# Reordering the start of a fused attention and FFN kernel: first loads, score tiles, one eviction and the weight slices

## The chip, the cores and the metric

The kernel runs on one core of a Trainium2 chip. The core has TensorE (PE in the profile; PEld is its weight load), VectorE (DVE), ScalarE (ACT), GpSimd (POOL) and SyncE (SP). Work between them is ordered by semaphores; each engine runs its own list in order. DMAs are issued by SP, ACT and POOL and are moved by 16 DMA engines. The metric is the device time of one execution in microseconds, median over runs. All times below are microseconds unless said otherwise; positions are counted from the start of the profiled span.

## The reference

The inputs are q, k, v of shape (8 batches, 12 heads, 448 positions, 64) and three weights. Attention uses a sigmoid in place of a softmax, and its output feeds a gated FFN:

```python
scores = (1 / sqrt(64)) * (q @ k.T) - log(448)
attn   = sigmoid(scores)
x      = (attn @ v) laid out as (8 * 448 tokens, 12 * 64 = 768)
g      = x @ w_gate                       # 768 -> 1536
out    = (g * sigmoid(g)) * (x @ w_val) @ w_out   # 1536 -> 768
```

The output is (3584, 768) in float32.

## The kernel before

**Groups and tiles.** The work of attention is cut into 24 groups n: batch n // 3, and four heads each. For one group the kernel loads q, k and v, casts q and k to bf16 (`cast`, L204; for the parts of group 0 `cast_part`, L174), transposes them in seven pieces of 128 columns on PE against an identity (`trans_part`, L223) and copies them from PSUM to SBUF (the tiles `T` and `Tk`, L229). Later groups are transposed by DMA instead. The keys of a group form seven chunks c. For each tile (n, c), `qk_tile` (L254) makes the scores of 64 keys by 448 queries for four heads, four matmul instructions on 64x64 weights, and `sig_tile` (L273) runs one sigmoid over 128 x 896 of them on ACT into `pt_a`. `chunk(n, c)` is both. When all seven tiles of a group exist, `pv(n)` multiplies them with V (L289, 28 matmuls) into one PSUM slot and evicts the slot to the FFN's input `xT`: bank 0 by one copy on DVE (L304), bank 1 by two copies that swap partition halves (L312).

**PSUM.** All of PSUM is a ring of four slots of two banks (`ring`, taken by `Banked`). A slot goes to the next user in the order in which the program asks, unless `at` names one; the new user's matmuls wait until the last reader of the former user is done. So a score tile has to wait for the sigmoid of the tile four uses earlier, and whoever follows a `pv` in a slot has to wait for its evictions.

**FFN.** `ffn1_mm` (L324) multiplies weights with `xT`, gate into bank 0, value into bank 1; each output column block f takes six products for each of the two. The weights come in four column slices, `wg` and `wv` 0 to 3, each for three blocks f. At the end of the ramp three blocks are begun early (`early[0]` to `early[2]`) with the four of six `xT` tiles that the first two groups give; the other two come from `pv(2)`. After that a planner's list alternates FFN1 blocks, attention visits of the next groups and, later, the third matmul. The list is the same before and after.

**The ramp's order.** Everything up to the early FFN1 blocks is written out by hand at the end of the function, one call after another, and each engine's list follows it. The four part loads of group 0 come first (`load_part`; q in pieces 0 to 3 and 4 to 6, k in pieces 0 to 1 and 2 to 6), then the loads of groups 1 to 3 on SP. Eight matmuls on a zero tile keep PE busy meanwhile (L814). Then the casts and transposes of group 0, chunks (0,0) and (0,1), the transposes of the second part of k, and so on; `trans_pe(n)` transposes a whole group and copies it on DVE.

**POOL's queue.** POOL issues the DMAs that change the type (V, the weight slices) and some loads of q and k (`load(n, which, G)`), and casts q and k of group 4 on (`casts`). It does this in program order, so a cast that waits for its load holds up the DMAs written behind it. `plan` lists such calls for later visits; the entry (3, 2) is carried out after tile (3, 2).

The ramp's slots come out as follows. Slots 0 and 1 hold the transposes of group 0; then tiles (0,0) to (0,5) take 2, 3, 0, 1, 2, 3; group 1's transposes 0; (0,6) 1; (1,0) 2; (1,1) 3; (1,2) 0; `pv(0)` 1; (1,3) 2; (1,4) 3; group 2's transposes 0; (1,5) 1; (1,6) 2; (2,0) 3; (2,1) 0; `pv(1)` 1; (2,2) 2; group 3's transposes 3; (2,3) 0; then (2,4) 2, `early[0]` 1, (2,5) 0, `early[1]` 3, (2,6) 2, `pv(2)` 0, `early[2]` 2.

Of the kernel before, what the change touches and what calls it, by code (L numbers as in the profile page):

```python
# [20 lines left out]
def kernel(  # L21
# [10 lines left out]
    nc = tc.nc  # L32
# [5 lines left out]
    C = S // D  # L38
# [35 lines left out]
    ring_at = [0]  # L74
# [42 lines left out]
    def apart(second, *firsts):  # L117

        for first in firsts:
            keys[0] += 1  # L120
            tc.add_to_no_dep_group(f"half{keys[0]}", first.ins)
            tc.declare_no_dep(second.ins, group=f"half{keys[0]}", reason="another bank or other partitions")
# [8 lines left out]
    def w_load(kind, i):  # L131
        cs = slice(i * FW * 128, (i + 1) * FW * 128)
        if kind == "o":
            rows = moe_w_out[i // 2 * 2 * FW * 128:(i // 2 + 1) * 2 * FW * 128, :]
            nc.gpsimd.dma_start(out=wo16[i], in_=rows.rearrange("(f h p) n -> h p f n", h=2, p=128)[i % 2])
        else:
            w, dst = (moe_w_gate, wg16[i]) if kind == "g" else (moe_w_val, wv16[i])
            nc.gpsimd.dma_start(out=dst, in_=w[:, cs].rearrange("(j p) n -> p j n", p=128))
# [23 lines left out]
    def load_part(n, which, eng, lo, hi):  # L162

        st = osp.tile([128, DM], FP32, tag="osb", name=f"st{which}_{n}_{lo}")[:, :2 * (hi - lo) * D]
        st = st.rearrange("p (h x) -> p h x", h=2)
        eng.dma_start(out=st, in_=src_of(n, which)[:, :, lo * D:hi * D])  # L166
        qkv_st[(n, which, lo)] = st
# [21 lines left out]
    def load_v(n):  # L189
        t = v16p.tile([128, 2, S], FP16, tag="v16", name=f"v16_{n}")  # L190
        if flip(n):
            b, j = divmod(n, NJ)
            src = v[b, 4 * j:4 * j + 4].rearrange("h (p c) d -> p h (c d)", c=C)
            for w, heads in enumerate((slice(0, 4, 3), slice(1, 3))):
                nc.gpsimd.dma_start(out=t[w * 64:(w + 1) * 64], in_=src[:, heads])
        else:
            nc.gpsimd.dma_start(out=t, in_=src_of(n, 2))
        v16[n] = t

    def cast(n, which, eng):  # L200
        st = qkv_st.pop((n, which))
        t = c16.tile([128, C, 2, D], BF16, tag="c16", name=f"c16_{which}_{n}")
        q16[(n, which, 0)] = t
        eng.tensor_copy(  # L204
            out=t.rearrange("p c h d -> p h c d"), in_=st.rearrange("p h (c d) -> p h c d", c=C)
        )
# [10 lines left out]
    def trans_part(D2, bank, n, which, lo, hi, eng, d):  # L217

        t = q16.pop((n, which, lo))
        ps = D2.t.bitcast(BF16).rearrange("p w (c i) -> p w c i", c=8)  # L220
        for c in range(hi - lo):
            D2.write(
                nc.tensor.transpose(out=ps[:, bank, c, :], in_=t[:, c].rearrange("p h d -> p (h d)"), identity=idn),  # L223
                bank,
            )

        def copy():
            f = eng.copy if eng is nc.scalar else eng.tensor_copy
            D2.read(f(out=d, in_=ps[:, bank, :hi - lo, :]), bank)  # L229
            for c in range(lo, hi):  # L230
                qT[(n, which, c)] = d[:, c - lo]

        return copy

    def trans_pe(n):
        D2 = Banked()
        ds = [qkT.tile([128, C, 128], BF16, tag=f"T{w}", name=f"T{w}_{n}") for w in range(2)]
        for f in [trans_part(D2, w, n, w, 0, C, nc.vector, ds[w]) for w in range(2)]:
            f()
        qT[(n, 0)] = ds[0]  # L240
# [5 lines left out]
    def qk_tile(n, c, at=None):  # L246
        sd = Banked(at=at)
        sc = sd.t
        qt, kt = qT[(n, 0)], qT[(n, 1, c)]
        for w in range(2):  # L250
            for h2 in range(2):
                r = slice(h2 * 64, h2 * 64 + 64)
                g = (w ^ (h2 and flip(n))) * 64
                nc.tensor.matmul(  # L254
                    out=sc[g:g + 64, h2, :S],
                    lhsT=kt[r, w * 64:(w + 1) * 64],
                    rhs=qt[r, :, w * 64:(w + 1) * 64],
                    start=True,
                    stop=True,
                )  # L260
        return sd

    def sig_tile(n, c, sd, split=False):
        sc = sd.t
        pt = pt_a[:, pt_at[0] % 10]
        pt_at[0] += 1
        if split:
            for h2 in range(2):
                sd.read(
                    nc.scalar.activation(out=pt[:, h2, :], in_=sc[:, h2, :S], func=SIGM, bias=sbias, scale=qkscale), h2  # L270
                )
        else:
            nc.scalar.activation(out=pt, in_=sc[:, :, :S], func=SIGM, bias=sbias, scale=qkscale)  # L273
        pts[(n, c)] = pt

    def pv(n, how=0, at=None):

        b, j = divmod(n, NJ)
        P = Banked(at=at).t
        vt = v16.pop(n)  # L280
        for c in range(C):
            pt = pts.pop((n, c))
            for h2 in range(2):
                for w in range(2):
                    r, g = w * 64, (w ^ h2) * 64
                    if flip(n):
                        r, g = g, r
                    r = slice(r, r + 64)
                    nc.tensor.matmul(  # L289
                        out=P[g:g + 64, h2, :S],  # L290
                        lhsT=vt[r, h2, c * D:(c + 1) * D],
                        rhs=pt[r, h2, :],
                        start=(c == 0),
                        stop=(c == C - 1),
                    )

        def x_tile(h2):
            if n >= NQ - NJ:
                at = 4 * W2 + (2 * j + h2) * S
                return half_of(stg_a)[:, at:at + S]  # L300
            return xtp.tile([128, S], FP16, tag="xT", name=f"xT_{b}_{2 * j + h2}")

        xs = [x_tile(h2) for h2 in range(2)]
        first = nc.vector.tensor_copy(out=xs[0], in_=P[:, 0, :S])  # L304
        pairs = [(xs[1], P[:, 1, :S])] if flip(n) else [
            (xs[1][w * 64:(w + 1) * 64, :], P[(1 - w) * 64:(2 - w) * 64, 1, :S]) for w in range(2)
        ]
        for o, i in pairs:
            if how == 2:
                apart(nc.scalar.copy(out=o, in_=i), first)  # L310
            else:
                nc.vector.tensor_copy(out=o, in_=i)  # L312
        for h2 in range(2):
            xT[(b, 2 * j + h2)] = xs[h2]

# [3 lines left out]
    def ffn1_mm(D, b, f, prs, banks=(0, 1)):  # L319
        cs = slice((f % FW) * 128, (f % FW) * 128 + 128)  # L320
        for i in banks:
            for pr in prs:
                D.write(
                    nc.tensor.matmul(  # L324
                        out=D.t[:, i, :S], lhsT=(wg16, wv16)[i][f // FW][:, pr, cs], rhs=xT[(b, pr)],
                        start=(pr == 0), stop=(pr == NP - 1),
                    ),
                    i,
                )
# [447 lines left out]
    for grp in visits:  # L777
        n, c = grp[0]
# [3 lines left out]
        else:  # L782
            at = n + (0.5 if c else 0.0)
# [19 lines left out]


    QS, KS = 4, 2
    load_part(0, 1, nc.scalar, 0, KS)
    load_part(0, 0, nc.sync, 0, QS)
    load_part(0, 0, nc.sync, QS, C)
    load_part(0, 1, nc.sync, KS, C)
    for n, which in ((1, 0), (1, 1), (2, 0), (2, 1), (3, 0), (3, 1)):  # L810
        load(n, which)
# [1 line left out]
    for i in range(8):  # L813
# [4 lines left out]
    dk = [qkT.tile([128, n, 128], BF16, tag=f"Tk{n}", bufs=1, name=f"Tk{n}") for n in (KS, C - KS)]  # L818
    dq = qkT.tile([128, C, 128], BF16, tag="T0", name="T0_0")
    Dk, Dq = Banked(), Banked()  # L820
    trans_part(Dk, 0, 0, 1, 0, KS, nc.scalar, dk[0])()
    copies = [
        trans_part(Dq, 0, 0, 0, 0, QS, V, dq[:, :QS]),
        trans_part(Dq, 1, 0, 0, QS, C, V, dq[:, QS:]),
    ]
    for f in copies:
        f()
# [39 lines left out]
    def chunk(n, c, at=None):  # L867
        sig_tile(n, c, qk_tile(n, c, at))
# [12 lines left out]
    w_load("v", 1)  # L881
    load(4, 0, G)
    load(4, 1, G)
    load_v(3)
    for c in range(2, 6):
        chunk(0, c)
    trans_pe(1)
# [2 lines left out]
    chunk(0, 6)  # L890
    for c in range(3):
        chunk(1, c)
    pv(0)
    chunk(1, 3)
    chunk(1, 4)
    trans_pe(2)
    cast(3, 0, V)
    cast(3, 1, V)
    load(5, 0, G)
    load(5, 1, G)  # L900
    load_v(4)
    w_load("g", 2)
    chunk(1, 5)
    chunk(1, 6)
    chunk(2, 0)
    chunk(2, 1)
# [1 line left out]
    chunk(2, 2)  # L908
    trans_pe(3)
    casts(4)  # L910
    w_load("v", 2)
    load_v(5)
    w_load("g", 3)
    w_load("v", 3)
    chunk(2, 3)
# [1 line left out]
    k0 = ring_at[0] % 4  # L917
# [4 lines left out]
    ffn1_mm(early[0], 0, 0, range(3), (0,))  # L922
    chunk(2, 5, at=(k0 + 3) % 4)
    ffn1_mm(early[0], 0, 0, (3,), (0,))
    ffn1_mm(early[0], 0, 0, four, (1,))
    chunk(2, 6, at=(k0 + 1) % 4)
    ffn1_mm(early[1], 0, 1, four, (0,))
    pv(2, how=2, at=(k0 + 3) % 4)
    ffn1_mm(early[1], 0, 1, four, (1,))
# [2 lines left out]
    for f, Df in enumerate(early):  # L932
# [5 lines left out]

    post = []
    plan = {  # L940
        (3, 2): ((casts, 5), (post.append, 4)),
        (3, 4): ((post.append, 5),),
        (4, 0): ((fetch, 6),),
        (4, 4): ((ready, 6), (load_qk, 7), (load_qk, 8)),
# [102 lines left out]
```

## Time and profile before

| | us |
|---|---|
| median of 4 runs | 399.98 (399.53 to 400.93) |
| the profiled execution's own time | 400.42 |
| its span (first to last instruction) | 398.5 |
| PE busy in the span | 388.4 (97%) |
| DVE busy | 251.5 (63%) |
| ACT busy | 237.3 (60%) |
| POOL busy | 124.0 (31%) |
| first FFN1 product | 22.15 |
| granted TensorE clock, mean of the span | 0.995 |

The profile is of one execution. A line of the chain gives the start, the length and what it is; a line of a timeline gives start, length, engine, line of the program, operation, output<-input, and in brackets the idle time before it with what ended it. A line of busy time by stretch gives the stretch and its length, the busy time and (x) instruction count of PE, PEld, DVE, ACT and POOL, then the granted clock, the share of the DMA engines' time and GB/s. Matmuls are pipelined and their ends are modelled, so a busy PE is not PE at its peak.

### The profile page before, as it was taken

The page shows a single profiled execution, that of the slowest core. Times are in us where ns is not written, and L with a number is a line of the kernel's source. Part 1 is how long each engine was busy: PE and PEld are TensorE (multiplying, and loading weights), DVE is VectorE, ACT ScalarE, POOL GpSimd, SP SyncE. Part 2 cuts the span into 40 slices and gives each one's busy share as a digit, 9 for nine tenths or more (in the row PEclk, how much of TensorE's full clock was granted, in tenths as well). Part 3 has the DMA queues.
Part 4 walks back from the last instruction along what each step waited for, and adds up shares of the span by engine and source line. Part 5 has one row for each costly group of instructions (what it writes and reads, how often), then busy time and mean ns, then how long its engine had stood idle before and what let it go on. Part 6 is the DMA issues. An engine that isn't in the chain of part 4 may idle for free.

```text
span 398.5 us, 8117 instructions
## 1 busy us (share of the span) xinstructions
PE 388.4 (97%) x3110; PEld 202.7 (51%) x3110; DVE 251.5 (63%) x504; ACT 237.3 (60%) x385; POOL 124.0 (31%) x204
## 2 busy tenths in 40 slices
PE   6899999999999999999999999999999999999995
PEld 2545445444555444444455555455556655555663
DVE  2737646688643454466675554799986558787553
ACT  4966795746466797779772557966653065656000
POOL 3639042421311353333337538600007400000900
PEclk9899999999999999999999999999999999999999
DMA  8999989997599777798778699000000520000055
GB/s 262 253 245 257 244 174 227 185 180 116 137 286 232 172 164 163 163 187 163 165 162 200 102 195 243 17 2 1 1 2 0 160 79 2 2 2 0 2 171 146
DMA packets 65590, 54.39 MB, mean 137 GB/s; under 512 B 36048, under 2 KB 61744, under 8 KB 65552
## 3 DMA queue, kind: packets, MB, share of 16 engines
q1 hardware_dynamic: 49264, 37.04, 38.1%
q0 software_dynamic: 15376, 15.34, 24.5%
q10 hardware_dynamic: 912, 1.51, 1.2%
q8 instruction: 24, 0.39, 0.4%
q14 instruction: 14, 0.11, 0.1%
HBM read 47.19 MB, written 11.01 MB: 146 GB/s over the span
## 4 chain that ended last, share of the span: by engine, by line
PE 93%; DMA 3%; DVE 2%; issue 0%; SPq 0%; ACT 0%; DVEq 0%
PE ps_D L324 31%; PE ps_D L633 23%; PE ps_D L460 22%; PE ps_D L254 9%; PE ps_D L289 8%; DMA out_dram<-osb 2%; DMA st<-in_k_dram 1%; PE ps_D L223 1%; DVE xT L312 0%; DVE T L229 0%; DVE xT L304 0%; DVE osb L646 0%; SPq L166 0%; DVE stg_a L646 0%; ACT pt_a L270 0%
## 5 line engine op out<-in xcount | busy, mean ns | idle before, releaser
L273 ACT ACTIVATE pt_a<-ps_D 128x896 f16<-128x896 f32 x148 | 127.2, 921 | 42.4 <-PE ps_D L254 40.8
L324 PE MATMUL ps_D<-xT,wg 128*128 128x448 f16 x312 | 69.0, 353 | 0.2
L324 PE MATMUL ps_D<-xT,wv 128*128 128x448 f16 x312 | 68.5, 352 | 0.0
L349 DVE TENSOR_TENSOR t<-ps_D,s 128x448 f16<-128x448 f32 x52 | 32.4, 624 | 54.4 <-ACT s L347 53.6
L470 ACT ACTIVATE snap<-ps_D 128x448 f32<-128x448 f32 x66 | 34.3, 541 | 29.0 <-PE ps_D L460 28.4
L254 PE MATMUL ps_D<-T,T 64*64 64x448 bf16 x644 | 44.1, 357 | 1.3 <-DVE T L229 0.9
L324 PEld LDWEIGHTS <-wv 128*128 128x128 f16 x312 | 30.5, 98 | 28.6 <-issue 0.4
L324 PEld LDWEIGHTS <-wg 128*128 128x128 f16 x312 | 27.8, 98 | 33.6 <-issue 11.7
L347 ACT ACTIVATE s<-ps_D 128x448 f16<-128x448 f32 x52 | 28.7, 552 | 22.6 <-PE ps_D L324 22.6
L633 PEld LDWEIGHTS <-S 128*128 128x128 f16 x312 | 30.2, 98 | 21.8 <-issue 2.2
L633 PE MATMUL ps_D<-ramp_a,S 128*128 128x384 f16 x234 | 40.5, 326 | 0.5 <-DVE osb L646 0.5
L204 POOL CAST c<-stg_a 128x896 bf16<-128x896 f32 x40 | 36.4, 936 | 13.0 <-DMA stg_a<-in_q_dram 12.3
L289 PE MATMUL ps_D<-pt_a,v 64*64 64x448 f16 x672 | 35.9, 349 | 0.0
L353 DVE SCALAR_TENSOR_TENSOR hT<-ps_D,t 128x448 f16<-128x448 f32 x52 | 32.5, 625 | 5.4
L651 DVE SCALAR_TENSOR_TENSOR osb<-ps_D,osb 128x384 f32<-128x384 f32 x40 | 22.3, 557 | 18.5 <-PE ps_D L633 16.2
L862 POOL CAST held<-S 128x1 bf16<-128x1 f16 x3 | 0.6, 189 | 106.2 <-ACT osb L644 55.7
L646 DVE TENSOR_SCALAR osb<-ps_D 128x384 f32<-128x384 f32 x37 | 20.6, 558 | 20.0 <-PE ps_D L633 16.3
L633 PEld LDWEIGHTS <-hT 128*128 128x128 f16 x228 | 22.1, 98 | 15.6 <-issue 1.2
L460 PE MATMUL ps_D<-xS,wv 128*128 128x448 f16 x132 | 28.6, 352 | 0.0
L862 POOL CAST held<-pt_a 128x1 bf16<-128x1 f16 x13 | 2.5, 190 | 82.5 <-ACT pt_a L273 82.5
L254 PEld LDWEIGHTS <-T 64*64 64x64 bf16 x644 | 15.5, 105 | 23.7 <-issue 16.6
L460 PE MATMUL ps_D<-xT,wg 128*128 128x448 f16 x132 | 26.8, 353 | 0.0
(109 smaller groups left out, 500.3 us busy)
## 6 DMA issues: line engine op xcount, KB each, us to landing
out_dram<-osb SPq DMA_DIRECT2D x45, 192.0 KB, 3.9
stg_a<-in_q_dram SPq DMA_DIRECT2D x18, 448.0 KB, 5.7
stg_a<-in_k_dram SPq DMA_DIRECT2D x18, 448.0 KB, 6.2
v<-in_v_dram POOLq DMA_DIRECT2D x38, 112.0 KB, 4.5
wg<-in_moe_w_gate_dram POOLq DMA_DIRECT2D x4, 576.0 KB, 11.9
wv<-in_moe_w_val_dram POOLq DMA_DIRECT2D x4, 576.0 KB, 12.6
wo<-in_moe_w_out_dram POOLq DMA_DIRECT2D x4, 576.0 KB, 8.4
stg_a<-in_q_dram POOLq DMA_DIRECT2D x3, 448.0 KB, 13.8
```

Of the source, the lines that this page charges most:

```text
L204: eng.tensor_copy(out=t.rearrange("p c h d -> p h c d"), in_=st.rearrange("p h (c d) -> p h c d", c=C))
L254: nc.tensor.matmul(out=sc[g:g + 64, h2, :S], lhsT=kt[r, w * 64:(w + 1) * 64], rhs=qt[r, :, w * 64:(w + 1) * 64], start=True, stop=True,)
L273: nc.scalar.activation(out=pt, in_=sc[:, :, :S], func=SIGM, bias=sbias, scale=qkscale)
L289: nc.tensor.matmul(out=P[g:g + 64, h2, :S], lhsT=vt[r, h2, c * D:(c + 1) * D], rhs=pt[r, h2, :], start=(c == 0), stop=(c == C - 1),)
L324: nc.tensor.matmul(out=D.t[:, i, :S], lhsT=(wg16, wv16)[i][f // FW][:, pr, cs], rhs=xT[(b, pr)], start=(pr == 0), stop=(pr == NP - 1),),
L347: D.read(nc.scalar.activation(out=s16, in_=D.t[:, 0, :S], func=SIGM), 0)
L349: D.read(nc.vector.tensor_tensor(out=t1, in0=D.t[:, 0, :S], in1=s16, op=MULT), 0)
L353: nc.vector.scalar_tensor_tensor(out=hT[(b // 2, f)][:, b % 2, :], in0=D.t[:, 1, :S], scalar=hsc(b // 2), in1=t1, op0=MULT, op1=MULT),
L460: nc.tensor.matmul(out=D.t[:, bank, :S], lhsT=W(f, j), rhs=X(j), start=(start and j == 0), stop=(stop and j == JT - 1), skip_group_check=True,
L470: D.read(nc.scalar.mul(out=o, in_=D.t[:, bank, :S], mul=scale), bank)
L633: nc.tensor.matmul(out=D.t[:, bank, :hw], lhsT=l, rhs=B_(i), start=(first and i == order[0]), stop=(i == order[-1]), skip_group_check=True,),
L651: D.read(nc.vector.scalar_tensor_tensor(out=o, in0=i, scalar=1.0 / hsc(pb), in1=o, op0=MULT, op1=ADD), bank)
```

## The change

The change touches the ramp's order and one line of the later plan. No computation is added or taken away.

- The four part loads of group 0 keep their sizes. The second part of q goes from SP's queue to ACT's; the first part of k goes from ACT's queue to SP's, behind the first part of q. The transposes of k's first part come after both of q's.
- The scores of tile (1,3) are issued ahead of `pv(0)`, its sigmoid after it. `pv(0)` evicts bank 0 at once; its two copies of bank 1 are put off until after the copies of group 2's transposes (`then`).
- One ring slot is skipped between tiles (1,5) and (1,6). From (1,3) on the slots are now: (1,3) 1, `pv(0)` 2, (1,4) 3, group 2's transposes 0, (1,5) 1, (1,6) 3, (2,0) 0, (2,1) 1, `pv(1)` 2, (2,2) 3, group 3's transposes 0, (2,3) 1, (2,4) 3, `early[0]` 2, (2,5) 1, `early[1]` 0, (2,6) 3, `pv(2)` 1, `early[2]` 3.
- The scores of tile (2,6) come ahead of the four value products of `early[0]` instead of behind them.
- On POOL, V of group 3 is issued after the casts of group 4 instead of before the loads of group 5; gate and value slice 2 follow the loads of group 5 directly; V of groups 4 and 5 is issued at the plan's entry (3, 2), after the casts of group 5.

```diff
-    def pv(n, how=0, at=None):
+    def pv(n, how=0, at=None, then=None):
...
-        for o, i in pairs:
-            if how == 2:
-                apart(nc.scalar.copy(out=o, in_=i), first)
-            else:
-                nc.vector.tensor_copy(out=o, in_=i)
+        def second():
+            for o, i in pairs:
+                if how == 2:
+                    apart(nc.scalar.copy(out=o, in_=i), first)
+                else:
+                    nc.vector.tensor_copy(out=o, in_=i)
+
+        if then is None:
+            second()
+        else:
+            then.append(second)
...
-    load_part(0, 1, nc.scalar, 0, KS)
+    load_part(0, 0, nc.scalar, QS, C)
     load_part(0, 0, nc.sync, 0, QS)
-    load_part(0, 0, nc.sync, QS, C)
+    load_part(0, 1, nc.sync, 0, KS)
     load_part(0, 1, nc.sync, KS, C)
...
-    trans_part(Dk, 0, 0, 1, 0, KS, nc.scalar, dk[0])()
     copies = [
         trans_part(Dq, 0, 0, 0, 0, QS, V, dq[:, :QS]),
         trans_part(Dq, 1, 0, 0, QS, C, V, dq[:, QS:]),
+        trans_part(Dk, 0, 0, 1, 0, KS, nc.scalar, dk[0]),
     ]
...
     load(4, 0, G)
     load(4, 1, G)
-    load_v(3)
...
     for c in range(3):
         chunk(1, c)
-    pv(0)
-    chunk(1, 3)
+    ahead = qk_tile(1, 3)
+    then = []
+    pv(0, then=then)
+    sig_tile(1, 3, ahead)
     chunk(1, 4)
     trans_pe(2)
+    for f in then:
+        f()
     cast(3, 0, V)
     cast(3, 1, V)
     load(5, 0, G)
     load(5, 1, G)
-    load_v(4)
     w_load("g", 2)
+    w_load("v", 2)
     chunk(1, 5)
+    ring_at[0] += 1
     chunk(1, 6)
...
     casts(4)
-    w_load("v", 2)
-    load_v(5)
+    load_v(3)
     w_load("g", 3)
     w_load("v", 3)
...
     ffn1_mm(early[0], 0, 0, (3,), (0,))
+    chunk(2, 6, at=(k0 + 1) % 4)
     ffn1_mm(early[0], 0, 0, four, (1,))
-    chunk(2, 6, at=(k0 + 1) % 4)
     ffn1_mm(early[1], 0, 1, four, (0,))
...
-        (3, 2): ((casts, 5), (post.append, 4)),
+        (3, 2): ((casts, 5), (load_v, 4), (load_v, 5), (post.append, 4)),
```

## The prediction

> **What bounds the kernel now.** I read the page's engine table first, then the chain that ended last in order of time, then the timelines of PE, ACT and POOL over the first 50 us, the DMA issues one by one, and busy time by stretch.
>
> ```profile
> PE 388.4 (97%) x3110; PEld 202.7 (51%) x3110; DVE 251.5 (63%) x504; ACT 237.3 (60%) x385; POOL 124.0 (31%) x204
> ```
>
> PE is idle for 10.1 of 398.5 us. The waits below put nearly all idle time that a ramp edit could reach ahead of 22.15 us, where FFN1's first product starts; from there PE has work without a break until long after the edited code. So this change can win or lose only by moving that 22.15, or by making PE wait later. The chain up to it:
>
> ```profile
> 1.76 5.15 DMA st<-in_k_dram
> 6.93 0.50 DVE c L174
> 8.05 0.50 DVE Tk L229
> 8.60 1.67 PE ps_D L254 x16
> ...
> 13.39 1.54 PE ps_D L289 x28
> ...
> 15.03 0.62 DVE xT L304
> ...
> 15.68 0.63 DVE xT L312
> ...
> 16.97 1.17 DVE T L229 x2
> ...
> 18.18 0.57 PE ps_D L254 x8
> 18.75 1.35 PE ps_D L289 x26
> ...
> 20.20 0.62 DVE xT L304
> 20.84 0.62 DVE xT L312
> 21.48 0.63 DVE xT L312
> 22.15 0.73 PE ps_D L324 x3
> ```
>
> To be seen: the start hangs on the second part of k (issued 1.76, landed 6.91). Later the first PV (L289), its three evictions on DVE, the transposed copies of group 2 (L229), two score tiles (L254), the second PV, its three evictions and then FFN1 (L324) follow each other with almost no slack. The ACT timeline gives the pace beside it:
>
> ```profile
> 6.65 1.73 ACT L273 ACTIVATE pt_a<-ps_D 128x896 f16<-128x896 f32 x2 [1.19 <-PE ps_D L254]
> 9.19 15.04 ACT L273 ACTIVATE pt_a<-ps_D 128x896 f16<-128x896 f32 x18 [0.81 <-PE ps_D L254]
> 24.67 0.92 ACT L273 ACTIVATE pt_a<-ps_D 128x896 f16<-128x896 f32 x1 [0.45 <-PE ps_D L254]
> ```
>
> ACT does 18 sigmoids back to back, 0.84 us each with three small gaps, 0.81 without. Each frees one of four PSUM slots, so PE cannot run its scores ahead of this pace. From narrow windows of this timeline I take the ends that matter: tile (0,6) 12.39 + 0.95 = 13.34, tile (1,0) 13.19 + 0.96 = 14.15, tile (1,2) 15.77, tile (1,4) 17.39. PE follows a freed slot by 0.05 (the transposes at 15.82 after 15.77).
>
> **First parts of q and k.** The change puts the 192 KB q part on ACT's queue at 0.74 instead of second on SP at 1.27, and the 128 KB k part second on SP instead of on ACT at 0.74. SP still issues three DMAs and ACT one, and k's long part stays third on SP at 1.76. The q part gains at most 0.53; the k part loses about as much. Its cast (ACT, 0.41), transposes and copy (ACT, 0.37) now stand last in PE's order, so the first score tile stays near 6.22 (5.8 to 6.4). Nothing comes of it: the first two sigmoids (6.65 to 8.38) end 0.81 before the third can start, and that waits for the long k part. Ahead of or beside that part lie the same 576 KB, 64 KB less of them on its own queue. At the 349 GB/s of the 5.27 to 8.69 row, 64 KB is 0.19 us: k's landing moves by -0.2 to +0.2. I take 0, since all four parts share the transfer rate. Here a rule speaks against the edit. The Trainium skill, "DMA: Bandwidth & Descriptors", section "Issuing engines are not separate DMA queues", says that issuing on several engines saves only the sequencer's issue time. By it too the sum would hold nothing for k's landing.
>
> **Scores (1,3) ahead of the first PV.** They take the slot that the PV had, free at 13.34, and run at 13.39. The PV now gets the slot of tile (1,0), whose sigmoid ends at 14.15: it starts at 14.20 instead of 13.39, 0.81 later. PE idles in between; behind the waiting PV stand tile (1,4) and group 2's transposes, and these wait for the slot of (1,2) until 15.82 anyway. V's landing (5.20 + 7.9 = 13.1) was just in time and is now covered.
>
> **Eviction in two goes.** Before, from the PV's start to the second PV's: 1.64 to the first eviction (13.39 to 15.03), 1.91 for three evictions, 0.03, 1.16 for two copies, 0.05, 0.41 for two score tiles: 5.20, hence 18.59. After: 14.20 + 1.64 = 15.84, first eviction to 16.46, copies (group 2's transposes run at 15.82 as before and are ready) 16.48 to 17.64, then the two deferred evictions, 1.26, to 18.90. The skipped ring slot gives the second PV the first PV's slot, so it waits for them: 18.95 against 18.59, **+0.36**. Holding two evictions back saves 0.45 of the chain, but its start is 0.81 later. Behind the waiting second PV stand tile (2,2), group 3's transposes and tile (2,3); ACT gets (2,2) at 20.7 and falls back into the pace it has now. Group 3's two casts (1.15) go behind them, to 20.05, still ahead of the second PV's end (20.44). Bounds: if the deferred evictions cost no wait, the next limit is tile (2,1), in the slot of (1,5). That sigmoid now has no gap before it and ends at 17.39 + 0.81 = 18.20; scores to 18.46, so -0.13. If no instruction on DVE overlaps the next, +0.5. I take +0.36, as the copies at 16.97 and the evictions at 15.68 are the very instructions.
>
> ACT's gaps ahead of (1,5), 0.14 in all, go, but nothing on PE waits for it: the last PV of the ramp starts at 25.35 and needs tile (2,6), done at 25.59, only for its last four products at 26.5.
>
> **Score tile (2,6) ahead of four FFN1 products.** The same instructions in another order. PE gets there at 22.15 + 0.36 + five products' and a tile's time = 23.68; the slot comes with sigmoid (2,4), at 23.67, so +0.04, between 0 and 0.3. The value slice these products need landed at 10.73 + 11.5 = 22.2.
>
> **Weight slices ahead of V.** POOL's queue:
>
> ```profile
> 16.50 0.72 POOL L197 DMA_DIRECT2D v<-in_v_dram  x1 [0.75 <-DMA v<-in_v_dram]
> ...
> 26.58 0.84 POOL L138 DMA_DIRECT2D wg<-in_moe_w_gate_dram  x1 [2.19 <-DMA wg<-in_moe_w_gate_dram]
> 30.53 0.93 POOL L204 CAST c<-stg_a 128x896 bf16<-128x896 f32 x1 [3.11 <-DMA stg_a<-in_q_dram]
> 31.67 0.94 POOL L204 CAST c<-stg_a 128x896 bf16<-128x896 f32 x1 [0.21 <-DMA stg_a<-in_k_dram]
> 32.55 0.82 POOL L138 DMA_DIRECT2D wv<-in_moe_w_val_dram  x1
> ```
>
> From the tenth transfer on, each issue here starts 0.3 to 0.6 after the landing of the one eight before it (16.50 after 9.18 + 7.0; 26.58 after 12.23 + 14.1). With V of groups 3 and 4 moved behind, gate and value slice 2 are issued near 22.8 and 23.7 instead of 26.58 and 32.55. Gain: value slice 2 landed at 32.55 + 9.2 = 41.75 and is first used at 42.87, so nothing waited, and nothing is won. Cost: V of group 3 leaves POOL behind the casts of group 4, near 32.6, after 16.50. By its landing the queue has moved all that it had by value slice 2's landing, less V of group 4; from 34.9 to 41.75 it moved 1376 KB, 201 KB per us, so V lands near 41.75 - 1.1 = 40.6, needed at 44.51. V of group 4 by the same count 49.07 - 1.1 = 47.9, needed at 52.15; group 5's at 49.1, needed at 62.07. POOL's casts of group 5 start near 35 instead of 36.19, and q and k of group 6, behind the same bytes, land at 50.7 and 52.0 as now. Zero, covered by 3.9 us.
>
> **Sum.** 0 + 0.36 + 0.04 + 0 = +0.4 on the profiled execution: 400.42 becomes 400.8 (its span 398.5, with 1.9 around it). That execution lay 0.44 above the median of the runs shown, so I forecast 399.98 + 0.4 = **400.4**, a change within 0.3% (1.2 us), about what a measurement of this kernel can tell from no change. Its own range is 399.8 to 401.0.
>
> **Rivals.**
>
> *Faster: the long k part lands early.* If it landed as fast as the q part of 192 KB did (3.4 us, so 5.16), sigmoid (0,2) would be limited by the second one, which ends at 8.0 if the first score tile comes at 5.8: 8.0 against 9.19, -1.2, and with +0.4 the kernel is at 399.2. It decides once k lands 0.4 earlier. Against it: same bytes, same issue time.
>
> *Slower: V of group 3 is late for its PV at 44.51.* It decides if the landing takes over 11.9 us from 32.6. V transfers took 7.0 to 16.1; the longest would put it at 48.7 and cost 4.2, a middling 14 us 2.1: 402.5. Against it: long landings are those with much queued ahead, and the count of bytes gives 8.
>
> *Slower: a second stretch at half clock.* The stretch 5.27 to 8.69, in which PE was busy 1.50 of 3.42, is followed by one at 0.50:
>
> ```profile
> 5.27:8.69 3.42, 1.50 (x23) 0.79 (x24) 1.67 (x4) 1.92 (x3) 1.19 (x2) 1.00 1.02 349
> 8.69:12.10 3.41, 3.41 (x34) 1.98 (x34) 1.67 (x3) 2.92 (x4) 3.41 (x5) 0.50 1.12 315
> ...
> 15.51:18.93 3.42, 2.26 (x38) 1.50 (x41) 3.35 (x7) 3.38 (x5) 0.96 (x2) 1.00 1.31 207
> ```
>
> 14 transposes took 1.68 in it and 0.94 at 15.82. A busy share of 44% trips it, 66% does not. The change adds PE idle time (13.75 to 14.20, 18.6 to 18.95, 22.1 to 22.5); I count 2.6 busy us in 12.10 to 15.51 and 2.7 in 15.51 to 18.93, 77% and 79%, so it should not trip. If it does over the second PV, that PV's 1.32 doubles: 401.7. The Trainium skill, "TensorE: Matmul & The Clock Gate", section "Part 1: The HAM clock gate", says that the clock is halved after an idle window of some 3.4 us and that the windows run free of the kernel. By the page's idle window the first dip should not be there at all, so here the row decides; by its free windows the dip shifts from run to run, in both kernels.
>
> **How the numbers follow.** Forecast 0.64; k early 0.14 (0.05 of it beyond 0.3%, by the 1.4 us over which the four runs scatter); V late 0.07; second dip 0.10; what no row shows 0.05, halved. Slower by over 0.3%: 0.07 + 0.10 + 0.02 = 0.19; faster 0.05 + 0.02 = 0.07; within, 0.74. The range reaches to the faster rival and the dip: 399.1 to 401.9.
>
> **What would show it.** In the changed kernel: the first PV near 14.2 after a wait on ACT; group 2's copies near 16.5; the second PV near 18.95, waiting for L312's later twin; FFN1's first product near 22.5 against 22.15; no wait of PE for V at 44.9 or for weights. The forecast is wrong if the first PV starts before 14, if the third sigmoid does not start near 9.2, or if PE waits anywhere from 25 to 62.

## The result and the profile after

The changed kernel takes 400.40 us (median of 51 runs, 399.62 to 402.81). The kernel before, run beside it, takes 399.61 (75 runs, 398.98 to 401.88). The ratio is 1.0021, 95% interval 1.0014 to 1.0027: +0.8 us, slower, but by less than 0.3%. So 400.4 was forecast and 400.4 was measured, but that they meet is luck. The forecast was added to the median of the four runs known then, 399.98, which lies 0.37 above the median of the 75. As a change, +0.4 was forecast and +0.8 came, and of its terms two did not come out; the experiments separate them.

The profiled execution of the changed kernel took 401.71, with a span of 399.6. It belongs to an upper group: 12 of the 51 executions lie at 401.63 or above, none between 400.90 and 401.63. The page's engine row:

```profile
PE 389.3 (97%) x3110; PEld 203.2 (51%) x3110; DVE 251.2 (63%) x504; ACT 237.5 (59%) x385; POOL 123.9 (31%) x204
```

PE has the same 3110 instructions and is busy 0.9 longer. The chain of the changed kernel, in order of time (start, length, what), to be read beside the chain shown in the prediction:

```profile
8.57 3.35 ACT pt_a L273 x4
...
13.59 2.83 PE ps_D L289 x26
...
17.51 0.36 DVE T L229
18.05 0.61 DVE T L229
18.70 0.63 DVE xT L313
19.34 0.63 DVE xT L313
20.01 1.54 PE ps_D L289 x28
21.58 0.62 DVE xT L304
...
23.52 0.73 PE ps_D L330 x3
```

In the changed kernel L313 is the put-off eviction (L312 before) and L330 is FFN1 (L324 before). The order is as written: first PV, group 2's copies, the two put-off evictions, second PV. Three numbers differ from the prediction. The third sigmoid starts at 8.57 and not at 9.19. The first PV takes 2.83 where it took 1.52. FFN1 starts at 23.52 and not at 22.5. Why the PV is longer stands in the busy time by stretch (stretch, its length, busy time and count of PE, PEld, DVE, ACT, POOL; then granted clock, DMA share, GB/s):

```profile
10.19:13.60 3.41, 1.96 (x30) 0.83 (x28) 2.55 (x4) 3.41 (x6) 3.41 (x5) 1.00 1.11 334
13.60:17.01 3.41, 3.41 (x35) 1.87 (x35) 0.48 (x1) 2.47 (x4) 1.26 (x2) 0.50 1.26 224
```

The stretch at half clock, which before had at 8.69 to 12.10, lies here on the first PV, right behind a stretch in which PE was busy 1.96 of 3.41.

From FFN1 on, PE of the changed kernel runs 1.37 behind PE of before. That lag stays constant to 113 us. At 121 us another 0.26 is added, and at 147 us another 0.22. At 235 us 0.65 comes back, for there PE of before waited once and PE of the changed kernel did not. The answer on PE's waits in before, 228 to 242 us:

```profile
PE ps_D L633 <- DVE osb L646: 0.5, 1, 0.5
```

Of all profiled executions (two here, twelve below) four have such a step at 235, of 0.20 to 0.65, and the step at 147 too is there in some and not in others, in kernels of both kinds. I did not find their cause and don't count them to the change. 1.37 + 0.26 + 0.22 - 0.65 = 1.2, the distance between the two spans.

### The profile page after: what moved, and what is told of

Its sections match the earlier page's. It is cut to its first block, busy times and chain, and to the rows that moved or that the text cites. A ratio compares the mean times of both kernels' runs of the same rounds, so it can differ in the third digit from the quotient of the medians.

```text
span 399.6 us, 8117 instructions
## 1 busy us (share of the span) xinstructions
PE 389.3 (97%) x3110; PEld 203.2 (51%) x3110; DVE 251.2 (63%) x504; ACT 237.5 (59%) x385; POOL 123.9 (31%) x204
## 4 chain that ended last, share of the span: by engine, by line
PE 92%; DMA 2%; ACT 2%; DVE 1%; issue 1%; POOL 0%; SPq 0%; DVEq 0%; POOLq 0%
PE ps_D L330 29%; PE ps_D L639 23%; PE ps_D L466 22%; PE ps_D L254 8%; PE ps_D L289 8%; ACT pt_a L273 2%; DMA T<-c 1%; DMA out_dram<-osb 1%; PE ps_D L223 1%; PE ps_D L820 1%; DVE xT L313 0%; POOL c L204 0%; DVE T L229 0%; DVE xT L304 0%; DVE osb L657 0%
## 5 line engine op out<-in xcount | busy, mean ns | idle before, releaser
L330 PE MATMUL ps_D<-xT,wg 128*128 128x448 f16 x312 | 69.0, 353 | 0.4 <-DVE xT L313 0.3
L330 PE MATMUL ps_D<-xT,wv 128*128 128x448 f16 x312 | 68.5, 353 | 0.0
L330 PEld LDWEIGHTS <-wg 128*128 128x128 f16 x312 | 27.9, 98 | 33.9 <-issue 11.8
L330 PEld LDWEIGHTS <-wv 128*128 128x128 f16 x312 | 30.4, 98 | 28.7 <-issue 0.6
L289 PE MATMUL ps_D<-pt_a,v 64*64 64x448 f16 x672 | 37.3, 359 | 0.9 <-DVE xT L313 0.4
L289 PEld LDWEIGHTS <-v 64*64 64x64 f16 x672 | 20.3, 109 | 13.8 <-issue 2.0
## 6 DMA issues: line engine op xcount, KB each, us to landing
stg_a<-in_q_dram POOLq DMA_DIRECT2D x3, 448.0 KB, 12.6
```

Of the source, the lines that this page charges most:

```text
L289: nc.tensor.matmul(out=P[g:g + 64, h2, :S], lhsT=vt[r, h2, c * D:(c + 1) * D], rhs=pt[r, h2, :], start=(c == 0), stop=(c == C - 1),)
L330: nc.tensor.matmul(out=D.t[:, i, :S], lhsT=(wg16, wv16)[i][f // FW][:, pr, cs], rhs=xT[(b, pr)], start=(pr == 0), stop=(pr == NP - 1),),
```

## The experiments

Three starts in each profile are compared: that of the third sigmoid (S3, set by the long k part or, where that lands early enough, by the second sigmoid), of the second PV, and of FFN1's first product. FFN1 - S3 is what the PV part alone can change; in before it is 22.15 - 9.19 = 12.96. Twelve kernels ran, four to a chip, each group beside 35 runs of before on the same chip (medians 400.03, 399.79 and 399.77). Absolute times are compared only within a chip.

Three accounts of the +0.8 stood against each other. By the prediction's own, the PV part costs 0.36 on the chain and all else is nothing. By the first rival, half of it or more is the half-clock stretch on the first PV, which a share of the executions meets. By the second, it is the later step at 121 us, with stores or something else behind it. The first four kernels take the parts singly, the others take one suspect away at a time.

### The four parts, one by one

The first part loads:

```diff
-    load_part(0, 1, nc.scalar, 0, KS)
+    load_part(0, 0, nc.scalar, QS, C)
     load_part(0, 0, nc.sync, 0, QS)
-    load_part(0, 0, nc.sync, QS, C)
+    load_part(0, 1, nc.sync, 0, KS)
```

(with the transposes of k's first part behind q's)

> The kernel before with the first change alone: second part of q on ACT's queue, first part of k second on SP's, its transposes behind q's. Chain theory (the whole loss comes from the first PV's later start and the put-off evictions): within 0.1% of before, -0.2 to +0.2 us, since k's long part is still third on SP's queue. Rival (the loads matter: k's long part landed at 6.46 in the changed kernel's profile against 6.91): 0.3 to 0.5 us faster, and the third sigmoid starts near 8.6 instead of 9.2 in the profile.

Measured: 399.46 beside 400.03, ratio 0.9990 [0.9982, 0.9999]. The loads alone make the kernel faster by 0.4, with an interval that reaches from 0.7 to almost 0; two kernels below that have the new loads and the first PV in its old place, on other chips, give 0.9988 and 0.9991. S3 is at 8.65, FFN1 at 21.61, so FFN1 - S3 is 12.96 as before. The median time from issue to landing of the parts, in the answer on DMAs from 0 to 6 us, before:

```profile
st<-in_k_dram SPq DMA_DIRECT2D x1, 320.0 KB, 5.1
```

and with the new loads alone:

```profile
st<-in_k_dram SPq DMA_DIRECT2D x1, 320.0 KB, 4.8
```

One pair proves little, as the landing scatters between executions. Over all profiles of this study the cast that follows k's landing starts at 6.75 on average in the four with the old loads (6.31 to 6.96) and at 6.39 in the ten with the new ones (6.09 to 6.94): 0.36 earlier, uncertain by some 0.17 (an estimate from the scatter within each kind). The cast of q's second part on POOL moves from 4.85 to 4.23 on average, and V of group 0, queued behind it, is issued as much earlier. Which of the two, k or V, brings the gain these runs do not separate: in two of the three profiles with the old loads and the old PV, the first PV waited for V.

The PV part:

```diff
-    pv(0)
-    chunk(1, 3)
+    ahead = qk_tile(1, 3)
+    then = []
+    pv(0, then=then)
+    sig_tile(1, 3, ahead)
     chunk(1, 4)
     trans_pe(2)
+    for f in then:
+        f()
...
     chunk(1, 5)
+    ring_at[0] += 1
     chunk(1, 6)
```

(with `then` in `pv` as in the change)

> The kernel before with the scores of tile (1,3) ahead of the first PV, the first PV evicted in two goes and one ring slot skipped, nothing else. Chain theory: it carries all of the loss, +0.36 us where no half-clock stretch lies on the first PV and about +1.5 to +2 where one does, so +0.6 to +0.9 us over many runs (1.0015 to 1.0022). Rival (loads or POOL's order carry part of it): under +0.3 us.

Measured: 399.99 beside 400.03, ratio 0.9998 [0.9990, 1.0007]. The profile does show the loss: FFN1 - S3 is 13.54, of which 0.2 comes from a half-clock stretch that ended inside the first PV (it took 1.72). The expected +0.6 to +0.9 did not come. That this kernel is nevertheless not slower than before has one part that can be seen in the next two kernels, which have the old loads and the old PV. There the first PV waited for V of group 0. In the POOL-order kernel, PE's timeline has

```profile
13.03 1.52 PE L289 MATMUL ps_D<-pt_a,v 64*64 64x448 f16 x28 [0.58 <-DMA v<-in_v_dram]
```

and in the (2,6) kernel the same wait is 0.26. A PV that starts 0.8 later doesn't wait there. So with the old loads the late start is partly free. By the three profiles of the old kind FFN1 - S3 is 12.96, 13.39 and 12.99, mean 13.11. Against 13.34 undisturbed, and with 0.26 at 121 us, +0.5 would still be due, and the interval ends at +0.3. The rest stays open.

POOL's order (V of group 3 behind the casts of group 4, the weight slices ahead, V of 4 and 5 at the plan's entry):

```diff
     load(4, 1, G)
-    load_v(3)
...
-    load_v(4)
     w_load("g", 2)
+    w_load("v", 2)
...
     casts(4)
-    w_load("v", 2)
-    load_v(5)
+    load_v(3)
...
-        (3, 2): ((casts, 5), (post.append, 4)),
+        (3, 2): ((casts, 5), (load_v, 4), (load_v, 5), (post.append, 4)),
```

> The kernel before with POOL's order changed alone: gate and value slice 2 right behind group 5's loads, V of groups 3, 4 and 5 later. Chain theory: no difference, within 0.1%; V of group 3 lands near 40.6 and its PV does not wait. Rival (a late V slice or a late load of group 6 costs time in runs that were not profiled): slower by 0.2 us or more.

Measured: 399.97, ratio 1.0002 [0.9993, 1.0011], and PE has no wait from 25 to 63 us. Nothing was won or lost.

Tile (2,6) ahead of the four value products:

```diff
+    chunk(2, 6, at=(k0 + 1) % 4)
     ffn1_mm(early[0], 0, 0, four, (1,))
-    chunk(2, 6, at=(k0 + 1) % 4)
```

> The kernel before with the scores of tile (2,6) ahead of the four value products of the first early block, nothing else. Chain theory: no difference, within 0.1% (0 to +0.3 us). Rival (PE waits there for the slot of tile (2,4)): +0.2 us or more, and the profile shows PE waiting for ACT ahead of those scores.

Measured: 399.84, ratio 1.0000 [0.9991, 1.0010]. From FFN1's first product to the first product of the second block it takes 24.24 - 21.89 = 2.35, and 24.49 - 22.15 = 2.34 before.

### The changed kernel again, and what fills its wait

The changed kernel itself, on another chip:

> The whole change once more, beside the next three on one chip. Clock theory (the late first PV thins PE out ahead of it, so that in some executions the half-clock stretch falls on that PV): two groups of times, about three in four near before (0 to +0.5 us) and one in four 1.7 to 2 us above those, all of these with a mean clock of 0.994 to 0.996; median 1.000 to 1.002 of before. Chain theory alone: one group, +0.4 us, whatever the clock.

Measured: 400.09 beside 399.79, ratio 1.0007 [0.9993, 1.0020]; two of 12 executions at 401.4 to 401.5, the rest at most 400.98. The profile fell in the lower group. Its PE timeline:

```profile
13.25 0.38 PE L254 MATMUL ps_D<-T,T 64*64 64x448 bf16 x4 [0.24 <-ACT pt_a L273]
14.06 1.52 PE L289 MATMUL ps_D<-pt_a,v 64*64 64x448 f16 x28 [0.43 <-ACT pt_a L273]
...
18.86 1.52 PE L289 MATMUL ps_D<-pt_a,v 64*64 64x448 f16 x28 [0.38 <-DVE xT L313]
...
22.38 0.73 PE L330 MATMUL ps_D<-xT,wg 128*128 128x448 f16 x3 [0.34 <-DVE xT L313]
```

S3 is 9.04 here. First PV 5.02 behind it (before 4.20: +0.82, predicted +0.81), second PV 4.80 behind the first (before 5.20: -0.40, predicted -0.45), FFN1 3.52 behind that (before 3.56). FFN1 - S3 is 13.34, **+0.38** against 12.96; predicted +0.36. The two rows that carry it are there: the first PV waits for a sigmoid, the second for the put-off eviction.

The same kernel with its score tiles doubled in the thin stretch ahead of the first PV (repeated work, written to the same place):

```diff
-    chunk(0, 6)
+    sig_tile(0, 6, qk_tile(0, 6, times=2))
     for c in range(3):
-        chunk(1, c)
-    ahead = qk_tile(1, 3)
+        sig_tile(1, c, qk_tile(1, c, times=2))
+    ahead = qk_tile(1, 3, times=3)
```

> The whole change, with the score matmuls of tiles (0,6) to (1,2) issued twice and those of (1,3) three times into the same place (the same values again, 6 x 4 instructions more, some 0.2 us of PE each, where PE waits for slots anyway). Clock theory: the group 1.7 to 2 us up disappears, hardly any execution after the ramp's start shows a half-clock stretch, and the kernel is 0.2 to 0.7 us faster than the whole change in spite of more work. Chain theory alone: same time as the whole change or up to 0.3 us slower.

Measured: 400.07, ratio 1.0010 [0.9998, 1.0022]; one of 11 executions above 401 (401.76). The median is that of the changed kernel (400.09); the expected gain of 0.2 to 0.7 did not come. In the profile the stretch ahead of the first PV is fuller and no stretch is at half clock, but the changed kernel's own profile on this chip has none either. The changed kernel, then the one with doubled scores:

```profile
9.42:12.83 3.41, 2.17 (x34) 1.35 (x31) 2.66 (x4) 3.41 (x5) 3.41 (x5) 1.00 1.12 325
9.14:12.55 3.41, 2.70 (x46) 1.75 (x47) 2.76 (x5) 3.41 (x6) 3.41 (x5) 1.00 1.12 318
```

The loads and the PV part together:

> The kernel before with two parts: the first loads, and the scores ahead of the first PV with the eviction in two goes. Clock theory: the loads bring k's long part and with it ACT's pace forward, PE waits more ahead of the first PV, so the two together show the slow group that neither alone showed; like the whole change within 0.1%. Sum theory (parts add: -0.4 and 0.0): 0.3 to 0.4 us faster than before and no slow group. If POOL's order or tile (2,6) is needed for the loss, also faster than before.

Measured: 400.19, ratio 1.0008 [0.9994, 1.0023]; three of 12 executions at 401.57 to 401.86. The profiled execution (401.66) is one of them, and its stretches repeat the changed kernel's own:

```profile
10.43:13.85 3.42, 1.97 (x28) 0.75 (x29) 2.15 (x4) 3.42 (x5) 3.42 (x5) 1.00 1.12 324
13.85:17.26 3.41, 3.41 (x38) 2.08 (x31) 0.62 (x1) 2.62 (x4) 1.66 (x3) 0.50 1.28 220
```

The first PV took 2.68, FFN1 - S3 is 14.96 (14.95 in the changed kernel's profile). Against 13.34 the stretch costs 1.6, near the distance between the two groups of times (means 401.89 and 400.20 in the changed kernel's 51 executions). So the half-clock stretch on the first PV, which covers that PV in both profiles taken in the upper group and in none taken in the lower one, is what I take the upper group for. Of the other executions the record has the time and the mean granted clock, not where a stretch lay. All 21 executions above 401.3, of the changed kernel and the twelve below, have a mean clock of 0.991 to 0.996, so a half-clock stretch somewhere, and none of the 113 at 0.997 or more lies above 400.62. Many with a low clock are not in the upper group.

How often it falls so: in the kernels with the new loads and the PV part (the changed kernel, its repetition, this one and the padded one below) 20 of 87 executions, 12 + 2 + 3 + 3; with the doubled scores (here and once more below) 1 of 23; in the six kernels without the PV part as it was changed none of 70; with the PV part but the old loads none of 11. If the doubled scores changed nothing, one or none of 23 would come about once in thirty, an estimate from the 21 of 110 of both kinds together. The kernel before is not free of such executions: of the 105 that ran beside the experiments four lie above 401.3, where the upper group begins, and one of the 75.

### The 121 us

In the five profiles so far of kernels with both evictions put off, an eviction of the third matmul on DVE starts 0.36 late. In before DVE's timeline (in brackets the idle time before) has

```profile
120.23 0.56 DVE L651 SCALAR_TENSOR_TENSOR osb<-ps_D,osb 128x384 f32<-128x384 f32 x1 [2.42 <-PE ps_D L633]
```

with PE's products as releaser, and with the PV part alone

```profile
121.25 1.11 DVE L657 SCALAR_TENSOR_TENSOR osb<-ps_D,osb 128x384 f32<-128x384 f32 x2 [2.79 <-DMA out_dram<-osb]
```

The eviction frees a slot for PE, which is 0.26 later from there on. The profile names a store as releaser here, and PE's products in two others of the five. But the delay is the same 0.36 to 0.38 in all five, wherever the stores land, and these have one row of DVE's trace less ahead of that eviction, 191 against 192 (186 and 187 in the expectation below, by another count). The missing row is no work, of which DVE has 504 instructions in both kernels: it is one of the separate instructions that only wait for a semaphore, ahead of the second PV's first eviction (L304). So I tested the place in DVE's stream by adding one instruction to the changed kernel, a memset of one column that nobody reads:

```diff
     nc.vector.memset(warm, 0.0)
+    nc.vector.memset(one.tile([128, 1], BF16, tag="pad", name="pad"), 0.0)
```

> The whole change plus one memset of one element per partition on DVE at the start. In the traces so far every kernel with the put-off evictions has one DVE instruction less (186 instead of 187 ahead of that place), and in all five of them a DVE eviction near 121 us starts 0.36 us late and PE waits about 0.1 us more and runs 0.26 us later from there on; in the five others it does not. Position theory (where the instruction lies in DVE's stream decides): the one more instruction puts it back, that eviction starts 2.43 after the one before it, and nothing is lost at 121 us: 0.26 us faster than the whole change. Rival (a late store holds it up): the loss at 121 us stays.

Measured: 399.79 beside 399.77, ratio 1.0004 [0.9988, 1.0019]. In its profile the delay is gone:

```profile
119.70 0.56 DVE L658 SCALAR_TENSOR_TENSOR osb<-ps_D,osb 128x384 f32<-128x384 f32 x1 [2.42 <-PE ps_D L640]
```

and PE's lag at 121 us is 0. One more instruction at the start removes a delay 120 us later, so the place in the stream decides, and not the store. DVE's rows in the traces, waits included, show how. In all fourteen profiles DVE pauses 0.40 to 0.42 ahead of the 192nd row of its stream. In the nine without the delay that row is the wait for PE's products, which then lasts some 2.5 instead of 2.85, so the pause is hidden in it. In the five it is the eviction itself: in the PV-part kernel the wait ends at 120.83 and the eviction starts at 121.25. What makes the pause no run shows. A fetch of instructions would fit: in all fourteen an 8 KB transfer on an instruction queue starts 1.2 to 2.7 behind it. The ratio is too wide to show 0.26 in the time. Three of 12 executions lie at 401.4 to 401.5, as expected if the two losses are independent.

With the pad and the doubled scores together:

> The whole change plus the one memset, plus the doubled and tripled score matmuls of tiles (0,6) to (1,3) in PE's idle time. Clock theory: against the version with the memset alone, the group 1.7 to 2 us up (about one execution in four) goes or nearly goes, and the median is 0 to 0.4 us lower; executions that show a half-clock stretch (mean clock 0.994 to 0.996) lie at most 0.7 us above the others. If the stretch does not come from PE's thin work ahead of the first PV, about one in four stays 1.7 us up.

Measured: 400.06 beside 399.77, ratio 1.0004 [0.9993, 1.0015], no execution above 401.02; the delay at 121 us is gone here too (2.43). The median is 0.27 above the padded kernel's, where 0 to 0.4 below it was expected; the mean, 400.16, is that of the padded kernel, 400.17. The profile has a half-clock stretch, from 8.10 to 11.51, behind one in which PE was busy 1.86 of 3.41 (4.69 to 8.10) and ahead of the first PV, which takes its 1.52. So the doubled scores do not keep the clock up everywhere, and they cost, over all executions, about what they spare in the few: they support the mechanism and are no remedy.

### The change without the PV part

Loads, (2,6) and POOL's order as in the change; `pv` and what stands around it as before. The lines are against the changed kernel.

```diff
-    ahead = qk_tile(1, 3)
-    then = []
-    pv(0, then=then)
-    sig_tile(1, 3, ahead)
+    pv(0)
+    chunk(1, 3)
     chunk(1, 4)
     trans_pe(2)
-    for f in then:
-        f()
...
-    ring_at[0] += 1
     chunk(1, 6)
```

> The whole change with the part on the first PV undone: the PV ahead of the scores of (1,3), its three evictions together, no skipped slot; loads, POOL's order and tile (2,6) as changed. Chain and clock theory: FFN1 starts 12.96 after the third sigmoid again, no loss at 121 us, no group of executions 1.7 us up; 0.3 to 0.5 us faster than before, as the loads alone. If the loss comes from the parts together, it stays near or above before.

Measured: 399.51 beside 399.77, ratio 0.9991 [0.9981, 1.0001], FFN1 at 21.45 (13.06 behind S3, the first PV having waited 0.28 for V), no execution above 400.67, and no delay at 121 us. Beside the loads alone (0.9990) nothing is different, beside the whole change 0.3% is by the long measurement (1.0021) and 0.16% by the short one (1.0007). With the new loads, the PV part carries the loss; with the old ones most of it did not show in the time.

### Two attempts at a better version

Loads as in the change; only the last eviction of the first PV is put off; the second PV takes the first one's slot ahead of tile (2,1):

```diff
+    then = []
+    pv(0, then=then)
     chunk(1, 3)
     chunk(1, 4)
     trans_pe(2)
+    for o, i in then:
+        nc.vector.tensor_copy(out=o, in_=i)
+    ring_at[0] += 1
...
     chunk(2, 0)
+    pv(1, at=2)
     chunk(2, 1)
-    pv(1)
+    ring_at[0] += 1
```

(in `pv`, `then` takes only the last pair)

> The first loads as changed, the first PV in its old place, of its three evictions only the last put off behind group 2's copies, and the second PV in the slot of tile (1,5), ahead of the scores of (2,1). By the chain's rows the second PV starts 0.34 us earlier against the third sigmoid's start than before (9.06 after it instead of 9.40), FFN1 12.6 after it instead of 12.96: 0.3 us better than the loads alone, 0.6 to 0.8 us (0.15 to 0.2%) faster than before. If the tighter chain thins PE out and draws a half-clock stretch onto a PV, slower than the loads alone.

Measured: 399.43 beside 399.79 (and 400.09 for the changed kernel on the same chip), ratio 0.9988 [0.9977, 0.9999], no execution above 400.51. It beats both kernels, but by no more than the loads alone do (0.9990). Its PE timeline:

```profile
13.04 1.52 PE L289 MATMUL ps_D<-pt_a,v 64*64 64x448 f16 x28 [0.42 <-DMA v<-in_v_dram]
...
17.72 1.52 PE L289 MATMUL ps_D<-pt_a,v 64*64 64x448 f16 x28 [0.15 <-ACT pt_a L273]
...
21.32 0.38 PE L254 MATMUL ps_D<-T,T 64*64 64x448 bf16 x4 [0.42 <-ACT pt_a L273]
21.63 0.74 PE L326 MATMUL ps_D<-xT,wg 128*128 128x448 f16 x3
```

The second PV comes 9.07 after S3 (9.40 before). But FFN1 - S3 is 12.98: a score tile waits 0.42 for ACT just ahead of FFN1, and the 0.33 is gone. ACT's pace is the next limit.

Then the V wait of 0.42 was taken away, by giving q and k of group 3 to POOL's queue:

```diff
-    for n, which in ((1, 0), (1, 1), (2, 0), (2, 1), (3, 0), (3, 1)):
+    for n, which in ((1, 0), (1, 1), (2, 0), (2, 1)):
         load(n, which)
...
     load_v(1)
+    load(3, 0, G)
+    load(3, 1, G)
     w_load("g", 0)
```

> The loads as changed, only the last of the first PV's evictions put off, the second PV ahead of the scores of (2,1), and in addition q and k of group 3 issued by POOL behind V of group 1 instead of by SP at 4.7 and 5.7. In the version without the last edit the first PV waited 0.42 us for V of group 0, landed at 13.0. With 0.9 MB less ahead of and beside it V should land near 12, the PV start 4.2 to 4.4 after the third sigmoid and FFN1 12.6 after it: 0.3 us faster than that version, 0.6 to 0.9 us faster than before. Against it: q and k of group 3 land later, and if they land after 18 the transposes of group 3 and then FFN1 are late; the gate and value slices 0 move behind them by about 0.9 MB.

Measured: 399.93 beside 399.77, ratio 0.9999 [0.9989, 1.0009]. The first PV no longer waits for V (12.68), and FFN1 starts at 21.45. But FFN1 - S3 is 12.98 again, not 12.6: the score tile just ahead of FFN1 waits 0.42 for ACT here too. And the value slice behind the two loads is late:

```profile
23.04 0.93 PE L326 MATMUL ps_D<-xT,wv 128*128 128x448 f16 x4 [0.24 <-DMA wv<-in_moe_w_val_dram]
```

One transfer's wait was exchanged for another's, and ACT's pace held FFN1 in both.

## Why the prediction was right, and where not

**The loads: taken as 0, measured -0.4.** This is the term that was mis-sized. The reasoning counted 64 KB less on the long part's own queue, and bounded k's landing by -0.2 and +0.2. By the means over the profiles it lands 0.36 earlier, outside that bound (though uncertain by some 0.17), and 0.53 for the q part (predicted "at most") became 0.62. The faster rival ("the long k part lands early") was right in kind and asked for 1.2 at most; about a third of it came. The Trainium skill, "DMA: Bandwidth & Descriptors", section "Issuing engines are not separate DMA queues", says that several issuing engines save only the issue time. The q part's 0.6 is of the size of one issue on SP (0.98 for two in before's SP timeline); that k gains too isn't settled by it or by the runs.

**The PV part: predicted +0.36, measured +0.38** in the executions without a half-clock stretch (FFN1 - S3 13.34, 13.34 and 13.35 in three profiles, 12.96 before). Its two halves, 0.81 later and 0.45 won back, measured 0.82 and 0.40. This chain of rows was the right way to price it. What it left out is that the late start costs less where the first PV waits for V anyway: with the old loads the part cost at most 0.3. Of the signs named, "first PV near 14.2" came at 13.59 with S3 0.62 earlier: the same distance. By the letter of the text, which called the forecast wrong if that PV started before 14 or S3 did not come near 9.2, the loads step had failed and was balanced by what follows.

**Tile (2,6): +0.04, measured +0.01. POOL's order: 0, measured 0**, with no wait of PE from 25 to 63 us, and V of group 3 never late. The times given for the queue held within 0.8 us. Its timeline in the changed kernel:

```profile
22.36 0.85 POOL L138 DMA_DIRECT2D wg<-in_moe_w_gate_dram  x1
23.55 0.83 POOL L138 DMA_DIRECT2D wv<-in_moe_w_val_dram  x1 [0.34 <-DMA v<-in_v_dram]
...
33.33 0.70 POOL L197 DMA_DIRECT2D v<-in_v_dram  x1
```

Predicted were 22.8, 23.7 and 32.6.

**The second half-clock stretch: given 1 chance in 10 and put on the second PV.** It comes on the first PV, in about one execution in four. The step that failed is the count of busy time ("2.6 busy us in 12.10 to 15.51 and 2.7 in 15.51 to 18.93"). It was made in the stretches as one profile happened to cut them. The cuts lie elsewhere in each execution: the half-clock stretch begins at 8.69, 13.60, 13.85, 7.90 and 8.10 in the five profiles that have one. Counted in a stretch that ends where the first PV starts, PE's idle time ahead of it leaves 1.96 of 3.41. The price (+1.3 for a PV) was near the measured 1.6. The Trainium skill, "TensorE: Matmul & The Clock Gate", section "Part 1: The HAM clock gate (the "warmup" mystery)", has the windows run free of the kernel, which the runs agree with (3.41 us, different cuts); its idle window is not what is seen here, where a stretch with 1.96 busy of 3.41 came ahead of half clock. The prediction quoted the free windows and then drew from them only that the stretch would shift, not that every stretch of 3.4 us along the changed part had to be counted.

**The 0.26 at 121 us** stood in no step. The prediction named what was moved on DVE, but not that the number of instructions in DVE's stream ahead of a later place, waits included, changes by it.

**The sum again, from the runs:** -0.4 (loads) + 0.38 (PV part) + 0.26 (121 us) + 0.39 (half clock on the first PV, 20/87 x 1.7) = +0.63. Measured: 0.21% of 399.61, +0.8, interval 0.56 to 1.08. The sum fits, but loosely, as the loads' term alone is known to 0.3 or 0.4, and in the PV part tested alone 0.2 or more of its loss stayed unexplained. So the change came out at twice the forecast, and no further off because an unforeseen gain of 0.4 met unforeseen losses of 0.65; that 400.4 itself was hit is owed to the four early runs, 0.37 above the long median. Within 0.3% was rightly the likeliest. Taken together, the change gives up in its PV part more than its loads win.

## What to carry to other kernels

Where a chain alternates between engines, add up the rows from one user of a PSUM slot to the next: a step that starts 0.81 later and returns 0.45 was priced to 0.02 that way. A landing that scatters by 0.8 us between executions is not to be read from one profile, neither as the term nor as its bound. When an edit thins out PE's work, count its busy time in every 3.4 us along that place and not only in the stretches that one profile shows, and weigh the loss by how often it falls there.

## What was not expected of the hardware

- The granted clock does not depend on the busy share of a stretch, as the profile shows it, alone. 3.41 us stretches at full clock with 1.50, 1.86, 1.96, 1.97 and 2.03 busy were followed by half clock (2.03 in the PV-part kernel, 4.49 to 7.90, whose half clock lasted two stretches), others with 1.84 (changed kernel on the second chip, 6.00 to 9.42) and 1.92 (POOL-order kernel, 7.41 to 10.83) were not. Of the stretches up to 20 us none with 2.05 or more was. The granted clock's changes lie whole multiples of 3.413 us apart in each trace (115 of them, 392.53, in those two), so their cuts are not off; what else counts stays open.
- DVE pauses some 0.4 us at one place of its instruction stream, ahead of the 192nd row of its trace, in all fourteen profiles. One instruction more or less ahead of it, if only a wait, decides whether the pause falls into a wait and costs nothing or onto an eviction, which is then 0.36 late. The Trainium skill, "Runtime: NRT & Kernel Launch", section "Instruction fetch mechanics", has instructions fetched in blocks, the crossing mostly hidden. Here a pause tied to the place in the stream is hidden in nine profiles and not in five; that it is a fetch was not shown.
- The releaser that a profile names can be beside the point: a store stood for the 2.79 us above, though the wait had ended 0.41 before the eviction started, and in two others of the five PE's products stood for the same 2.78 and 2.80.
